# Three VectorE steps instead of four to turn fp64 weights into fp32, and full-height tail products

## The chip, the cores and the metric

One core of a Trainium2 chip runs one program: attention, a gated MLP over tokens and channels, and an MLP mixer, for a batch of four. The metric is the device time of one execution, in microseconds (us); lower is better. The engines are TensorE (PE; its weight loads are PEld), VectorE (DVE), ScalarE (ACT), GpSimd (POOL) and SyncE (SP, which issues the DMAs). Each works through its own list of instructions in order and waits on semaphores of the others.

## The reference, cut to what matters

```python
# attention: 4 batches, 8 heads, 1152 keys, 64 channels a head; queries are averaged in pairs (576)
scores = 1/sqrt(64) * q_pool @ k.T;  x = softmax(scores) @ v          # -> x: 4 x 576 x 512
# gated MLP
h = gelu(x @ w_in);  u, v = h[..., :512], h[..., 512:]
v_n = (v - mean(v)) / sqrt(var(v) + 1e-6) * g_ln
v_s = einsum('ts,bsd->btd', w_sg, v_n) + b_sg[None, :, None]          # 576 x 576 over tokens
x = x + (u * v_s) @ w_out
# mixer
h = maximum(x.T @ w_tok1, 0) @ w_tok2;  u = x + h.T                   # over tokens, 576 -> 256 -> 576
out = u + maximum(u @ w_ch1, 0) @ w_ch2
```

The weights `w_in`, `w_out`, `w_tok1`, `w_tok2`, `w_ch1` and `w_ch2` come as 64-bit floats and reach the kernel as 64-bit integers. `w_sg` is 32-bit.

## The kernel before

Every factor of a matmul is held as two fp32r tiles, a rounded high part and the rest (low), and a product is three matmuls: high by high, high by low, low by high (`products`, L203). The kernel has three stages in time.

*Attention* takes 16 pairs of a batch and two heads, some 32 us each. Its order on all engines is made by `Plan` (L62): every task has an engine, a duration, tasks that it follows and an urgency, and `run` places them one by one. PE's order is written out (`line`). DVE takes row maxima of scores (`mx`, L541), which PE waits for when its PSUM tiles run out; ACT takes exponentials (`e`, L592); POOL adds them up (`acc`, L598).

*The gated MLP* (`spatial`, L935) runs for each batch b: V (`psv`, L991), U (`psu`, L1057), the gate S over tokens (`pss`, `sg_mm`, L1075) in four blocks db, and the output product (`psz`/`pso`, L1099) of the batch before, after V. Each gate block is followed by a chain: DVE `gt` (L1084), POOL `gt` (L1087), ACT `g` (L1089), DVE `g` (L241). The order is that of the code; between its steps stand hooks, which `HOOKS` (L31) fills by name with other work. A "c" in it is one call of `feed.ops(1)`.

*The mixer* (`mixing`) has for each batch two blocks `psr` (`k1_mm`, L1256) with a relu split `r` into high (ACT, L1245) and low (DVE, L1246), then four blocks `psh` (L1266); after about 868 us come the channel products `psc` and `po`.

**The conversion.** A `Piece` (L251) is up to 128 x 512 weights: loaded by SP into `ws`, then turned into an fp32 tile `z` by bit operations on the upper word `top` and the lower word `low` of each number. `early` is two ACT instructions that make `d` (`wd`), the distance of the exponent from the middle; `step1` to `step4` are DVE instructions, the last of which takes numbers too small to zero by `d`. `high` (ACT, a cast) and `low_part` (POOL, a subtraction) split `z`. There are 42 pieces. Twelve are tasks of the plan (`conversion`); the other 30 go through `Feed`, whose generator `steps` yields after `step1` with `early`, after `step2` and after `step3`, and does the rest in a fourth call, so that a piece takes four calls of `ops`.

**The tail.** The 576 tokens are four tiles of 128 rows and a tail of 64. The tail tile of a token factor holds the high part in one half of its rows and the low part in the other, and the weight's high part stands in both halves, so that one 128-row matmul does two of the three products (`tail_products` leaves the third out). The matmul with the weight's low part (`sw` = 1) takes only the 64 rows with the high part: one matmul in 14, in `sg_mm` (4 batches x 4 blocks x 2 halves = 32) and in `k1_mm` (4 batches x 2 blocks = 8).

Of the kernel before, what the change touches and what calls it, by code (L numbers as in the profile page):

```python
# [11 lines left out]
F32 = mybir.dt.float32  # L12
F32R = mybir.dt.float32r
F16 = mybir.dt.float16
I32 = mybir.dt.int32
I64 = mybir.dt.int64
# [5 lines left out]
EXPMASK = 0x7F800000  # L22
# [125 lines left out]
def kernel(  # L148
# [16 lines left out]
    nc = tc.nc  # L165
# [20 lines left out]
    ident_r = const.tile([P, P], F32R, name="ident_r")  # L186
    ones = const.tile([P, P], F32, name="ones")
    m1024 = const.tile([P, 1], F32, name="m1024")
# [59 lines left out]
    class Piece:  # L248
# [17 lines left out]
        def early(self):  # L266
            self.d = d = self.cut(cvp.tile([P, 512], F16, tag="wd", name="wd", bufs=1))
            nc.scalar.activation(out=d, in_=self.top, func=AF.Abs, scale=2.0 ** -20)
            nc.scalar.activation(out=d, in_=d, func=AF.Abs, bias=m1024[:self.r])


        def step1(self):
            self.z = self.cut(cvp.tile([P, 512], F32, tag="wz", name="wz"))
            nc.vector.tensor_scalar(
                out=self.z.bitcast(I32), in0=self.top, scalar1=0x07FFFFFF, scalar2=3,
                op0=ALU.bitwise_and, op1=ALU.logical_shift_left)

        def step2(self):
            zi = self.z.bitcast(I32)
            nc.vector.scalar_tensor_tensor(  # L280
                out=zi, in0=self.low, scalar=29, in1=zi,
                op0=ALU.logical_shift_right, op1=ALU.bitwise_or)

        def step3(self):
            zi = self.z.bitcast(I32)
            nc.vector.scalar_tensor_tensor(  # L286
                out=zi, in0=self.top, scalar=-0x40000000, in1=zi,
                op0=ALU.bitwise_and, op1=ALU.bitwise_or)

        def step4(self):  # L290

            nc.vector.scalar_tensor_tensor(  # L292
                out=self.z, in0=self.d, scalar=127.0, in1=self.z, op0=ALU.is_le, op1=ALU.mult)
# [39 lines left out]
    class Feed:  # L333
# [16 lines left out]
        def steps(self, x):  # L350
            x.step1()
            x.early()
            yield
            x.step2()
            yield
            x.step3()
            yield
            x.step4()
            x.high()
            x.low_part()  # L360
            if x.away:
                for s in range(2):
                    x.send(s)
# [31 lines left out]
    def attention():  # L395
# [13 lines left out]
        for h in range(2):  # L409
            nc.vector.memset(f32(pick[D * h:D * h + 2]), 1.0)  # L410
        eps = keep.tile([P, 1], F32, name="eps", bufs=1)
# [204 lines left out]
        def sums(i, x):  # L616
            s = st[i][x]
            pt = bank()
            for h in range(2):
                nc.tensor.matmul(  # L620
                    pt[D * h:D * h + D, 0:TC], ones[:, 0:D], s.acc[:, h], start=True, stop=True)
            return pt
# [154 lines left out]
        for name, n in dict(ws=2, wd=1, wz=2, wn=1).items():  # L777
            plan.ring(name, n)
# [5 lines left out]
        def conversion(x, u):  # L784
            a = plan.add("SP", 0.05, lambda: x.load(nc.sync), after=[mark(u)], urgency=u - 20,
                         take=["ws"], land=4.0)
            d1 = plan.add("DVE", 1.0, x.step1, after=[a], urgency=u, take=["wz"])
            e = plan.add("ACT", 1.4, x.early, after=[a], urgency=u, take=["wd"])
            d2 = plan.add("DVE", 1.7, x.step2, after=[d1], urgency=u + 0.5)
            d3 = plan.add("DVE", 1.1, x.step3, after=[d2], urgency=u + 1)  # L790
            d4 = plan.add("DVE", 1.5, x.step4, after=[d3, e], urgency=u + 1.5,
# [138 lines left out]
    def spatial(fin, early):  # L930
# [221 lines left out]
        for b in range(B):  # L1152
# [15 lines left out]
            if last:  # L1168
# [6 lines left out]
                for j in range(JB):  # L1175
# [3 lines left out]
                todo.append(Piece(  # L1179
                    w_tok1[n0:T].rearrange("(a p) n -> p a n", p=TAIL),  # L1180
                    lambda: [x[r:r + TAIL, NTT - 1:NTT] for x, r in (
                        (L.wk1[0], 0), (L.wk1[1], 0), (L.wk1[0], TAIL))]))
# [18 lines left out]
    def mixing(L, fin):  # L1201
# [47 lines left out]
        def k1_mm(b, jb):  # L1249
# [113 lines left out]
    with tc.manual_schedule():  # L1363
        make_identity(nc, ident)
        nc.vector.tensor_copy(ident_r, ident)
        nc.vector.memset(ones, 1.0)
        nc.vector.memset(m1024, -1024.0)
        nc.scalar.copy(m1024, m1024)
        mixing(*spatial(*attention()))
# [31 lines left out]
```

## Time and profile before

| what | value |
|---|---|
| median of 3 runs | 1190.45 us (1186.25 to 1191.25) |
| the profiled execution | 1187.83 us, of which the span of instructions is 1186.0 us |
| busy over the span | PE 96%, PEld 79%, DVE 59%, ACT 38%, POOL 48% |
| granted TensorE clock, mean | 0.986 of full speed |
| mean of one conversion instruction, 128 x 512 | DVE 0.53, 0.88, 1.14 and 0.90 us; ACT 0.67 and 0.72 us |
| shortest and longest of step 3 (L286) | 0.42 and 1.83 us |

PE is busy nearly throughout, but a busy PE may be one whose matmuls start further apart than they need, and the rest of the question is where PE stands still and for whom. Rows of the timeline merge consecutive instructions of a line; the distance from the start of one row to the start of the next, divided by the count, is the time that one matmul takes of PE.

### The profile page before, as it was taken

Reading aid. Unit: us, or ns where it says so; the run is one execution under the profiler, and the core shown is the slowest. Engines: PE = TensorE matmul, PEld = TensorE weight load, DVE = VectorE, ACT = ScalarE, POOL = GpSimd, SP = SyncE. Lnnn points to the kernel's source line nnn. Section 1 sums busy time; section 2 is a strip of 40 time slices with the busy share of each in tenths; the row PEclk is TensorE's granted clock in tenths of the full one; section 3 lists DMA queues with packets and bytes.
Section 4 is the critical chain, followed back from the end, with each engine's and each line's share of the span. In section 5 each row is a group of like instructions: output and inputs, shape, how many; then the busy total and the mean of one; then the engine's idle time right before and its main releaser. Section 6 shows DMA issues by size and latency. Waiting matters only on the chain.

```text
span 1186.0 us, 22019 instructions
## 1 busy us (share of the span) xinstructions
PE 1139.7 (96%) x9249; PEld 938.8 (79%) x9249; DVE 700.2 (59%) x987; ACT 455.0 (38%) x821; POOL 571.7 (48%) x398
## 2 busy tenths in 40 slices
PE   5999999999999999998989999879999999999998
PEld 5777777777777777766879898867799888999887
DVE  5788888887676777746666666888841111212111
ACT  2355555454444555553434343445521111111111
POOL 2688888887777788783524342432240111110000
PEclk9999999999999999998999999989999999999999
DMA  8222234433334232117020201132230000000000
GB/s 180 42 66 69 78 79 107 120 81 79 80 91 99 72 83 67 57 54 252 29 79 20 88 18 54 54 98 89 89 143 19 19 19 10 18 10 19 18 19 18
DMA packets 81971, 79.68 MB, mean 67 GB/s; under 512 B 42192, under 2 KB 67024, under 8 KB 80592
## 3 DMA queue, kind: packets, MB, share of 16 engines
q1 hardware_dynamic: 81872, 78.28, 23.1%
q8 instruction: 72, 1.18, 0.4%
q14 instruction: 27, 0.22, 0.1%
HBM read 62.51 MB, written 15.76 MB: 66 GB/s over the span
## 4 chain that ended last, share of the span: by engine, by line
PE 74%; DVE 16%; ACT 4%; issue 3%; POOL 3%; DMA 0%; SPq 0%; DVEq 0%; POOLq 0%; ACTq 0%
PE sT L584 14%; PE psc L1319 13%; PE po L1339 13%; PE po L607 12%; PE s L534 10%; DVE mx L541 2%; PE pss L1075 2%; DVE wz L286 2%; PE psu L1057 2%; PE tt L483 2%; PE psz L1099 1%; POOL gt L1087 1%; DVE wz L280 1%; DVE wz L292 1%; PE pt L620 1%
## 5 line engine op out<-in xcount | busy, mean ns | idle before, releaser
L598 POOL TENSOR_TENSOR acc<-acc,e 128x576 f32<-128x576 f32 x224 | 322.2, 1439 | 75.2 <-ACT e L592 62.4
L541 DVE TENSOR_REDUCE mx<-s 128x2 f32<-128x768 f32 (+1 forms) x240 | 215.6, 945 | 90.9 <-PE s L534 90.9
L592 ACT ACTIVATE e<-sT 128x576 f32<-128x576 f32 x288 | 169.8, 651 | 96.0 <-PE sT L584 89.5
L584 PE MATMUL sT<-q,k 64*128 64x288 f32 x1728 | 167.7, 305 | 0.7 <-DVE mx L541 0.3
L584 PEld LDWEIGHTS sT<-q,k 64*128 64x128 f32 x1728 | 129.2, 186 | 43.5 <-DVE mx L541 16.6
L607 PE MATMUL po<-e,vn 128*64 128x288 f32 x1152 | 160.8, 414 | 0.0
L1319 PEld LDWEIGHTS psc<-x,w 128*128 128x128 f32 x1296 | 155.9, 189 | 0.7
L1319 PE MATMUL psc<-x,w 128*128 128x256 f32 x1296 | 156.3, 282 | 0.0
L1339 PE MATMUL po<-w,gc 128*128 128x512 f32 x648 | 153.3, 396 | 0.0
L534 PE MATMUL s<-k,q 64*128 64x384 f32 (+1 forms) x1440 | 147.7, 346 | 3.2 <-ACT k L516 1.1
L1339 PEld LDWEIGHTS po<-w,gc 128*128 128x128 f32 x648 | 120.8, 188 | 28.9
L1245 ACT ACTIVATE gc<-psc 128x256 fp32r<-128x256 f32 x108 | 41.6, 385 | 244.2 <-PE psc L1319 244.2
L534 PEld LDWEIGHTS s<-k,q 64*128 64x128 f32 (+1 forms) x1440 | 112.2, 179 | 21.0 <-ACT e L592 3.4
L607 PEld LDWEIGHTS po<-e,vn 128*64 128x64 f32 x1152 | 74.3, 136 | 57.5 <-issue 17.3
L1246 DVE SCALAR_TENSOR_TENSOR gc<-psc,gc 128x256 fp32r<-128x256 f32 x108 | 45.9, 425 | 108.1 <-ACT gc L1245 108.1
L237 POOL TENSOR_SCALAR x<-xT 128x1024 fp32r<-128x1024 f32 x9 | 9.8, 1088 | 198.6 <-PE psc L1319 198.1
L1346 DVE TENSOR_TENSOR ob<-po,us 128x512 f32<-128x512 f32 x18 | 12.4, 692 | 145.7 <-PE po L1339 145.7
L584 PE MATMUL sT<-nmT,pick 64*128 64x288 f32 x576 | 85.6, 292 | 0.0
L631 DVE RECIPROCAL pt<-pt 128x288 f32<-128x288 f32 x32 | 62.7, 1961 | 26.2 <-ACT pt L627 26.1
L1075 PE MATMUL pss<-wsg,vn 128*128 128x288 f32 x448 | 73.0, 310 | 3.8 <-POOL vn L241 3.8
L1075 PEld LDWEIGHTS pss<-wsg,vn 128*128 128x128 f32 x448 | 62.4, 188 | 14.0 <-issue 4.8
L241 POOL TENSOR_TENSOR vn<-gv,vn 128x512 fp32r<-128x512 f32 (+1 forms) x20 | 27.1, 1367 | 72.2 <-ACT vn L1041 69.8
(111 smaller groups left out, 1491.1 us busy)
## 6 DMA issues: line engine op xcount, KB each, us to landing
ws<-in_moe_w_ch_dram SPq DMA_DIRECT2D x24, 512.0 KB, 3.6
qn<-in_q_dram SPq DMA_DIRECT2D x32, 288.0 KB, 5.1
kn<-in_k_dram SPq DMA_DIRECT2D x32, 288.0 KB, 4.3
vn<-in_v_dram SPq DMA_DIRECT2D x32, 288.0 KB, 3.3
out_dram<-ob SPq DMA_DIRECT2D x18, 256.0 KB, 2.0
ws<-in_moe_w_in_dram SPq DMA_DIRECT2D x8, 512.0 KB, 4.8
ac<-ws SPq DMA_DIRECT2D x16, 256.0 KB, 2.4
w<-ac SPq DMA_DIRECT2D x4, 1024.0 KB, 8.7
```

What stands on the lines that cost most here:

```text
L534: nc.tensor.matmul(ps[0:m, h, 0:KC], flat(c.q[x])[r, t * P:t * P + m], c.k[y][r, cs], start=(n == 0), stop=(n == 2))
L541: nc.vector.tensor_reduce(out=mx[i % 2][0:m, t, :, g], in_=ps[0:m, :, 0:KC], axis=AX.X, op=ALU.max, negate=True)
L584: nc.tensor.matmul(ps[:, h, 0:TC], left, right, start=(n == 0), stop=(n == 3))
L592: nc.scalar.activation(out=s.e[j], in_=ps[:, :, 0:TC], func=AF.Exp)
L598: eng.tensor_tensor(out=s.acc, in0=s.e[0] if j == 1 else s.acc, in1=s.e[j], op=ALU.add)
L607: nc.tensor.matmul(s.po[D * h:D * h + D, 0:TC], c.vn[:, h, j], s.e[j][:, h], start=(j == 0), stop=(j == J - 1))
L631: nc.vector.reciprocal(out=s.den, in_=s.den)
L1075: nc.tensor.matmul(ps[:, ch, 0:TC], V[sx][r, ti, db * P:(db + 1) * P], L.ws[sw][r, ti, ch * TC:(ch + 1) * TC], start=first, stop=end)
L1245: nc.scalar.activation(out=h_, in_=ps, func=AF.Relu)
L1246: nc.vector.scalar_tensor_tensor(out=l_, in0=ps, scalar=0.0, in1=f32(h_), op0=ALU.max, op1=ALU.subtract)
L1319: nc.tensor.matmul(ps, WC1[f // 4][sw][:, cc, (f % 4) * P:(f % 4 + 1) * P], u[sx][:, cc], start=first, stop=end)
L1339: nc.tensor.matmul(pos[tt], g[sx][:, f, tt * P:(tt + 1) * P], WC2[f // 4][sw][:, f % 4], start=(f == 0 and n == 0), stop=(f == NF - 1 and ...
```

## The change

The three DVE steps now are: `step1` shifts the upper word with one bit flipped, `step2` masks the result and ORs in `y`, `step3` takes the minimum with the largest fp32 and multiplies by `d`. `y` (new tile `wy`) holds the top three bits of the lower word and is made by one ACT instruction (`early`); `d` is now the sign of a scaled upper word, made by two ACT instructions (`signs`, with the function Sign). Both are called in the piece's first call, after `step1`. The piece still takes four calls: the third now holds the last DVE step, and the fourth only the split. In the plan the low bits stand ahead of the signs, with durations 0.7 and 1.4. The tail matmuls with the weight's low part take all 128 rows, and for the mixer POOL sets the lower 64 rows of that tile to zero. The constants `ident_r` and `ones` are made inside the attention stage, and `m1024` is gone.

```diff
         def early(self):
+            self.y = y = self.cut(cvp.tile([P, 512], I32, tag="wy", name="wy", bufs=1))
+            nc.scalar.activation(out=y, in_=self.low.bitcast(U32), func=AF.Copy,
+                                 scale=2.0 ** -29 * (1 - 2.0 ** -20), bias=-0.5 + 2.0 ** -22)
+
+        def signs(self):
             self.d = d = self.cut(cvp.tile([P, 512], F16, tag="wd", name="wd", bufs=1))
-            nc.scalar.activation(out=d, in_=self.top, func=AF.Abs, scale=2.0 ** -20)
-            nc.scalar.activation(out=d, in_=d, func=AF.Abs, bias=m1024[:self.r])
+            nc.scalar.activation(out=d.bitcast(I16), in_=self.top.bitcast(F32), func=AF.Copy,
+                                 scale=TINY)
+            nc.scalar.activation(out=d, in_=d.bitcast(I16), func=AF.Sign)
...
             nc.vector.tensor_scalar(
-                out=self.z.bitcast(I32), in0=self.top, scalar1=0x07FFFFFF, scalar2=3,
-                op0=ALU.bitwise_and, op1=ALU.logical_shift_left)
+                out=self.z.bitcast(I32), in0=self.top, scalar1=0x08000000, scalar2=3,
+                op0=ALU.bitwise_xor, op1=ALU.logical_shift_left)
...
             nc.vector.scalar_tensor_tensor(
-                out=zi, in0=self.low, scalar=29, in1=zi,
-                op0=ALU.logical_shift_right, op1=ALU.bitwise_or)
+                out=zi, in0=zi, scalar=0x7FFFFFFF, in1=self.y,
+                op0=ALU.bitwise_and, op1=ALU.bitwise_or)
...
         def step3(self):
-            zi = self.z.bitcast(I32)
             nc.vector.scalar_tensor_tensor(
-                out=zi, in0=self.top, scalar=-0x40000000, in1=zi,
-                op0=ALU.bitwise_and, op1=ALU.bitwise_or)
-
-        def step4(self):
-            nc.vector.scalar_tensor_tensor(
-                out=self.z, in0=self.d, scalar=127.0, in1=self.z, op0=ALU.is_le, op1=ALU.mult)
+                out=self.z, in0=self.z, scalar=HUGE, in1=self.d, op0=ALU.min, op1=ALU.mult)
...
             x.step1()
             x.early()
+            x.signs()
             yield
             x.step2()
             yield
             x.step3()
             yield
-            x.step4()
             x.high()
             x.low_part()
...
-            e = plan.add("ACT", 1.4, x.early, after=[a], urgency=u, take=["wd"])
...
+            y = plan.add("ACT", 0.7, x.early, after=[a], urgency=u, take=["wy"])
+            e = plan.add("ACT", 1.4, x.signs, after=[a], urgency=u + 1, take=["wd"])
...
-                    r = high_rows(b, ti) if sw else slice(0, P)
                     nc.tensor.matmul(
-                        ps[:, ch, 0:TC], V[sx][r, ti, db * P:(db + 1) * P],
-                        L.ws[sw][r, ti, ch * TC:(ch + 1) * TC], start=first, stop=end)
+                        ps[:, ch, 0:TC], V[sx][:, ti, db * P:(db + 1) * P],
+                        L.ws[sw][:, ti, ch * TC:(ch + 1) * TC], start=first, stop=end)
...
+                def tail_dst():
+                    nc.gpsimd.memset(f32(L.wk1[1][TAIL:P, NTT - 1:NTT]), 0.0)
+                    return [x[r:r + TAIL, NTT - 1:NTT] for x, r in (
+                        (L.wk1[0], 0), (L.wk1[1], 0), (L.wk1[0], TAIL))]
...
-                r = slice(0, TT[ti][1] if sw else P)
                 nc.tensor.matmul(
-                    ps, wk1[sw][r, ti, jb * P:(jb + 1) * P], c.y[sx][r, ti],
+                    ps, wk1[sw][:, ti, jb * P:(jb + 1) * P], c.y[sx][:, ti],
                     start=first, stop=end)
```

What this moves is seen best on DVE. In the first gate stage (batch 0), from the first block's chain to the second's; `wz` is the piece's fp32 tile, `gt` and `g` the gate's. Before:

```order
L280 SCALAR_TENSOR_TENSOR wz<-ws,wz 128x512
L1084 SCALAR_TENSOR_TENSOR gt<-pss,g_half,b_bc 128x2x288
L286 SCALAR_TENSOR_TENSOR wz<-ws,wz 128x512
L241 TENSOR_TENSOR g_7607<-gt,g_7606 128x576
L292 SCALAR_TENSOR_TENSOR wz<-wd,wz 128x512
L274 TENSOR_SCALAR wz<-ws 128x512
```

The same stretch now:

```order
L289 SCALAR_TENSOR_TENSOR wz<-wz,wy 128x512
L1090 SCALAR_TENSOR_TENSOR gt<-pss,g_half,b_bc 128x2x288
L295 SCALAR_TENSOR_TENSOR wz<-wz,wd 128x512
L241 TENSOR_TENSOR g_7616<-gt,g_7615 128x576
L282 TENSOR_SCALAR wz<-ws 128x512
```

The step that completes the piece stood behind `g` and now stands ahead of it, and one step is gone.

In the last gate stage (batch 3), one block's chain to the next. Before:

```order
L1084 SCALAR_TENSOR_TENSOR gt<-pss,g_half,b_bc 128x2x288
L280 SCALAR_TENSOR_TENSOR wz<-ws,wz 128x512
L286 SCALAR_TENSOR_TENSOR wz<-ws,wz 128x512
L292 SCALAR_TENSOR_TENSOR wz<-wd,wz 128x512
L241 TENSOR_TENSOR g_7607<-gt,g_7606 128x576
L274 TENSOR_SCALAR wz<-ws 128x512
```

The same stretch now:

```order
L1090 SCALAR_TENSOR_TENSOR gt<-pss,g_half,b_bc 128x2x288
L289 SCALAR_TENSOR_TENSOR wz<-wz,wy 128x512
L295 SCALAR_TENSOR_TENSOR wz<-wz,wd 128x512
L241 TENSOR_TENSOR g_7616<-gt,g_7615 128x576
L282 TENSOR_SCALAR wz<-ws 128x512
```

Three conversion steps between `gt` and `g` have become two.

In the mixer's first batch, around the two relu splits `r`. Before:

```order
L274 TENSOR_SCALAR wz<-ws 128x512
L280 SCALAR_TENSOR_TENSOR wz<-ws,wz 128x512
L286 SCALAR_TENSOR_TENSOR wz<-ws,wz 128x512
L1246 SCALAR_TENSOR_TENSOR r_9780<-psr,r_9779 128x512
L292 SCALAR_TENSOR_TENSOR wz<-wd,wz 128x512
L1246 SCALAR_TENSOR_TENSOR r_9780<-psr,r_9779 128x512
```

The same stretch now:

```order
L282 TENSOR_SCALAR wz<-ws 128x512
L289 SCALAR_TENSOR_TENSOR wz<-wz,wy 128x512
L295 SCALAR_TENSOR_TENSOR wz<-wz,wd 128x512
L1254 SCALAR_TENSOR_TENSOR r_9811<-psr,r_9810 128x512 x2
L241 TENSOR_TENSOR y_9851<-pty,y_9850 128x512 x3
```

The last conversion step has moved from between the two `r` to ahead of both. PE's matmuls keep their order in all these stages.

## Rows read from the trace of the kernel before

**Rows 1.** Windows by stage: length, each engine's busy us (instructions), clock, DMA.
```profile
35.00:535.00 500.00, 497.87 (x5228) 367.27 (x5226) 381.81 (x451) 252.85 (x450) 408.25 (x275) 1.00 0.31 79
...
600.00:800.00 200.00, 182.64 (x1159) 166.38 (x1157) 137.07 (x220) 80.63 (x129) 78.07 (x61) 0.96 0.17 57
800.00:868.00 68.00, 63.81 (x364) 52.53 (x364) 59.05 (x86) 34.67 (x60) 19.10 (x13) 1.00 0.25 78
```

**Rows 2.** Timeline of PE: start, us, instructions, [idle before <-releaser].
```profile
635.51 18.15 PE L1075 MATMUL pss<-wsg,vn 128*128 128x288 f32 x112
653.50 14.32 PE L991 MATMUL psv<-w,x 128*128 128x512 f32 x60
667.65 3.35 PE L1099 MATMUL pso<-g,wo 128*128 128x288 f32 x24
...
684.07 12.89 PE L1057 MATMUL psu<-x,w 128*128 128x288 f32 x96
696.79 18.09 PE L1075 MATMUL pss<-wsg,vn 128*128 128x288 f32 x112
...
783.34 4.09 PE L1099 MATMUL pso<-g,wo 128*128 128x288 f32 x18 [3.56 <-ACT g L1089]
...
817.22 7.47 PE L1256 MATMUL psr<-y,x 128*128 128x512 f32 x28
824.53 1.69 PE L1238 MATMUL pty<-ident,xT 128*128 128x128 f32 x12
```

**Rows 3.** Groups by form, conversion: count | busy us, mean ns of one | idle before.
```profile
L286 DVE SCALAR_TENSOR_TENSOR wz<-ws,wz 128x512 int32<-128x512 int32 x38 | 43.3, 1139 | 0.5
...
L292 DVE SCALAR_TENSOR_TENSOR wz<-wd,wz 128x512 f32<-128x512 f16 x38 | 34.2, 899 | 1.2
L280 DVE SCALAR_TENSOR_TENSOR wz<-ws,wz 128x512 int32<-128x512 int32 x38 | 33.2, 875 | 0.9
...
L269 ACT ACTIVATE wd<-wd,m 128x512 f16<-128x512 f16 x38 | 27.5, 724 | 1.2
...
L268 ACT ACTIVATE wd<-ws 128x512 f16<-128x512 int32 x38 | 25.5, 671 | 0.0
...
L274 DVE TENSOR_SCALAR wz<-ws 128x512 int32<-128x512 int32 x38 | 20.0, 526 | 0.1
```

**Rows 4.** Waits of PE from 600 to 872 us: total, times, longest.
```profile
PE psv L991 <- ACT x L384: 3.1, 1, 3.1
...
PE psz L1099 <- DVE gv L927: 1.8, 1, 1.8
...
PE pso L1099 <- ACT g L1089: 7.9, 2, 4.4
PE pss L1075 <- POOL vn L241: 2.9, 1, 2.9
PE psh L1266 <- ACT r L1245: 2.7, 4, 1.0
PE psh L1266 <- DVE r L1246: 1.3, 1, 1.3
```

**Rows 5.** Timeline of the last gate stage on DVE, ACT and POOL.
```profile
773.64 0.81 DVE L1084 SCALAR_TENSOR_TENSOR gt<-pss,g_half,b_bc 128x576 f32<-128x576 f32 x1
...
775.09 1.77 DVE L286 SCALAR_TENSOR_TENSOR wz<-ws,wz 128x512 int32<-128x512 int32 x1
776.96 0.69 DVE L292 SCALAR_TENSOR_TENSOR wz<-wd,wz 128x512 f32<-128x512 f16 x1
...
780.19 0.80 DVE L1084 SCALAR_TENSOR_TENSOR gt<-pss,g_half,b_bc 128x576 f32<-128x576 f32 x1
...
777.68 0.62 ACT L302 CAST x<-wz 128x512 fp32r<-128x512 f32 x1 [4.38 <-DVE wz L292]
...
774.60 1.71 POOL L1087 TENSOR_TENSOR gt<-gt,gu 128x576 f32<-128x576 f32 x1 [1.82 <-DVE gt L1084]
```

**Rows 6.** Groups by form, the one load of ACT's function table.
```profile
L1368 ACT ACT_TABLE_LOAD x1 | 1.3, 1283 | 0.7 <-PEq L1385 0.7
```

More of the change, by code (lines that the diff above doesn't have):

```diff
@@ L14 @@
 F16 = mybir.dt.float16
+I16 = mybir.dt.int16
 I32 = mybir.dt.int32
+U32 = mybir.dt.uint32
 I64 = mybir.dt.int64
@@ L20 @@
 PSUM = bass.MemoryType.PSUM
-EXPMASK = 0x7F800000
+HUGE = float(np.finfo(np.float32).max)
+TINY = 2.0 ** 14 / 1.0625
 C1 = float(np.float32(np.sqrt(2.0 / np.pi)))
@@ L185 @@
     ident = const.tile([P, P], F32, name="ident")
-    ident_r = const.tile([P, P], F32R, name="ident_r")
-    ones = const.tile([P, P], F32, name="ones")
-    m1024 = const.tile([P, 1], F32, name="m1024")
     xT = const.tile([P, CC, NT], F32, name="xT")
@@ L410, in attention @@
             nc.vector.memset(f32(pick[D * h:D * h + 2]), 1.0)
+        ident_r = ld.tile([P, P], F32R, name="ident_r")
+        nc.vector.tensor_copy(ident_r, ident)
+        ones = keep.tile([P, D], F32, name="ones", bufs=1)
+        nc.vector.memset(ones, 1.0)
         eps = keep.tile([P, 1], F32, name="eps", bufs=1)
@@ L620, in sums @@
                 nc.tensor.matmul(
-                    pt[D * h:D * h + D, 0:TC], ones[:, 0:D], s.acc[:, h], start=True, stop=True)
+                    pt[D * h:D * h + D, 0:TC], ones, s.acc[:, h], start=True, stop=True)
             return pt
@@ L776, in attention @@
             tasks(i)
-        for name, n in dict(ws=2, wd=1, wz=2, wn=1).items():
+        for name, n in dict(ws=2, wd=1, wy=1, wz=2, wn=1).items():
             plan.ring(name, n)
@@ L786, in conversion @@
                          take=["ws"], land=4.0)
-            d1 = plan.add("DVE", 1.0, x.step1, after=[a], urgency=u, take=["wz"])
-            e = plan.add("ACT", 1.4, x.early, after=[a], urgency=u, take=["wd"])
-            d2 = plan.add("DVE", 1.7, x.step2, after=[d1], urgency=u + 0.5)
-            d3 = plan.add("DVE", 1.1, x.step3, after=[d2], urgency=u + 1)
-            d4 = plan.add("DVE", 1.5, x.step4, after=[d3, e], urgency=u + 1.5,
+            d1 = plan.add("DVE", 0.9, x.step1, after=[a], urgency=u, take=["wz"])
+            y = plan.add("ACT", 0.7, x.early, after=[a], urgency=u, take=["wy"])
+            e = plan.add("ACT", 1.4, x.signs, after=[a], urgency=u + 1, take=["wd"])
+            d2 = plan.add("DVE", 1.3, x.step2, after=[d1, y], urgency=u + 1, give=[("wy", y)])
+            d4 = plan.add("DVE", 1.3, x.step3, after=[d2, e], urgency=u + 1.5,
                           give=[("wd", e)] + ([] if x.away else [("ws", a)]))
@@ L1178, in spatial @@
                                       dst([w[:, 0:n0 // P] for w in L.wk1], P, c)))
[L1179 to L1182, printed above, removed]
+                def tail_dst():
+                    nc.gpsimd.memset(f32(L.wk1[1][TAIL:P, NTT - 1:NTT]), 0.0)
+                    return [x[r:r + TAIL, NTT - 1:NTT] for x, r in (
+                        (L.wk1[0], 0), (L.wk1[1], 0), (L.wk1[0], TAIL))]
+                todo.append(Piece(w_tok1[n0:T].rearrange("(a p) n -> p a n", p=TAIL), tail_dst))
                 for j in range(3):
@@ L1364 @@
         make_identity(nc, ident)
[L1365 to L1368, printed above, removed]
         mixing(*spatial(*attention()))
```

## The prediction

> **What bounds the kernel now.** I read the busy time by stage first, then the timeline of PE for how far apart its matmuls start, then the waits of PE, and last the chains that those waits lead back to. By stage, PE is busy for 497.87 of 500 us of attention, for 182.64 of the 200 us from 600 on, and for 63.81 of 68 us of the mixer's token part, where DVE is busy for 59.05 [rows 1]. So PE sets the time nearly everywhere, and what can be won is of two kinds: matmuls that start further apart than they must, and the waits of PE in the MLP and the mixer.
>
> The first kind shows where the halved matmuls are. The gate stage of batch 1 has 112 matmuls of 288 columns and runs without a pause from 635.51 to 653.50, 17.99 us; batch 2's U stage, 96 matmuls of the same width, takes 12.72 us, 0.1325 each [rows 2]. At that rate 112 would take 14.84. The gate stage is 3.15 us longer and has 8 matmuls with 64 rows: 0.39 us each. In the mixer 28 matmuls of 512 columns take 7.31 us, against 28 x 0.2358 = 6.60 at the rate of the 60 matmuls `psv` (14.15 us), which is 0.71 for 2 of them, 0.35 each [rows 2]. Two stages of different width give nearly the same excess per 64-row matmul, so it goes with the change of height and not with the columns.
>
> The second kind: PE waits 3.1 us for an ACT split of x after gate stage 0, 1.8 for DVE's gelu after stage 1, 2.9 for POOL's normalized v before stage 3, 7.9 for ACT's g after it, and 2.7 + 1.3 for the relu splits in the mixer [rows 4]. The chain behind the 7.9 is in the rows of the last gate stage: `gt` on DVE at 773.64 and the next one only at 780.19, a period of 6.55 us although PE needs about 4.5 per block. Within it step 3 takes 1.77 and step 4 0.69, and ACT's cast, idle 4.38 us for step 4, stands ahead of ACT's g [rows 5].
>
> **The change part by part.** *Tail matmuls.* 32 in the gate and 8 in the mixer take 128 rows: 4 x 3.15 + 4 x 0.71 = 15.4 us less of PE time. A matmul of 128 rows in the same place costs the common 0.13 or 0.24; the smallest saving is none, if the excess is not from the height, the largest 15.4. I take 15.4, since it repeats at both widths. Whether it reaches the end depends on the waits behind each stage.
>
> The Trainium skill speaks of this twice, in opposite directions: "TensorEngine Tiling (Array Packing)", Theoretical Speedup, gives contractions of at most 64 rows up to twice the speed when tiled, and Key Properties says that a change of tiling mode drains TensorE. By the first, full height would win nothing (that is the fourth rival); by the second, each lone 64-row matmul pays on the way in and out. The excess of 0.39 us [rows 2] is on the side of the second.
>
> *DVE.* Four steps average 0.53 + 0.88 + 1.14 + 0.90 = 3.44 us a piece [rows 3]. Gone is one of three SCALAR_TENSOR_TENSOR; the two that stay have new operations and one contiguous operand instead of a strided one, which the trace doesn't show: between the 0.69 of an undisturbed one and the 1.77 of one beside a running POOL instruction [rows 5]. I take old prices for them, and for the one removed 0.69 in a chain, 0.97 (the mean of the three) in sum: 42 x 0.97 = 41 us less of DVE, of which most lies beside PE work.
>
> The Trainium skill, "SBUF — State Buffer", Who interferes with whom, says that a DVE instruction with two SBUF inputs is blocked for the whole of a GpSimd instruction that reads SBUF. Step 3 started at 775.09 and ended 0.55 us after POOL's `gt` (774.60 for 1.71) [rows 5], which agrees. By this rule the step after the removed one inherits the block, so that a chain gains 0.69 and not 1.77.
>
> *ACT.* One more instruction per piece, priced as its neighbours at 0.67 (0.72 as the other end) [rows 3]: 28 us in all. It is hidden where ACT waits anyway, as for step 4 above (4.38 us idle), and costs up to 0.67 where an x split or a relu stands behind it. New waits: step 2 for `y`, step 3 for the signs, up to 0.67 + 0.67 + 0.72 = 2.06 us after the piece's first call. Behind them on DVE stand `gt`, relu lows and, in attention, row maxima.
>
> *Order.* The last step is now one call earlier. Where ACT's cast follows, z is ready when ACT comes to it, and g, x splits and relus behind the cast go at once. POOL's zeroing is one small instruction where POOL is idle. SP issues the same DMAs; a few in attention change places, and PE does not wait for DMAs there.
>
> Now by place, each with its bounds. A chain gains 0.79 by the first block (two tail matmuls sooner), and 0.69 to 1.8 for each conversion in it.
> - Stage 0: three conversions, 0.79 + 2.1 = 2.9 to 6.2. All that PE could use is 3.15 + 3.1. I take 4 (0 to 6.25).
> - Stage 1: three conversions, the same; PE could use 3.15 + 1.8. I take 4 (0 to 5).
> - Stage 2: two conversions, and `y` stands ahead of x splits that POOL does before its `gt`: 0.79 + 1.4 - 0.67 = 1.5 to 3.6. I take 2 (0 to 3.6).
> - Stage 3: 0.79 + 2.1 by the chain, and 1 of the wait for v, whose cast stands behind a conversion's. I take 4 (0 to 3.15 + 2.9 + 7.9 = 14).
> - Mixer, token part: 2.8 of matmuls, and 2.7 of the 4.0 us of waits, since the cast that held up the second relu is done before it. Three pieces a batch need some 3.4 us each by ACT (2.06, then a DVE step of 0.69, then the cast 0.62), as much as before by DVE, so not all goes. I take 5.5 (2.8 to 6.8).
> - Attention: 2.1 us of idle in all [rows 1], some of it behind conversions. I take 1 (from 4 lost, by new waits, to 2.1 won).
>
> The sum is 4 + 4 + 2 + 4 + 5.5 + 1 = 20.5 us. The profiled execution took 1187.83, so 1167.3; the median of the runs is 2.6 us above that execution, and with it the sum gives 1170.0. I forecast 1169. All lower ends together give 1.2 us lost, all upper ends 37.7 won: 1150 to 1192.
>
> **The rivals.** *The waits eat PE's gain.* ACT's extra instruction takes the place of DVE's, the chains stay as long as they were, and PE comes earlier to the same waits. Then only the mixer's 2.8, about 0.8 a stage by the earlier first block and perhaps 2 of the order remain: 8 us, 1181. For it: four of five gate and mixer waits are for ACT or DVE chains [rows 4]. Against: ACT's idle 4.38 us before the cast [rows 5], three times what it gets to do.
>
> *More than the sum.* After the long waits PE is slow: 18 matmuls from 783.34 took 4.09 us, 0.227 each against 0.1325 [rows 2]. If the waits shrink, this goes too, 1.7 us there, and steps save 1.8 rather than 0.69 in the chains: about 30 us, 1159.
>
> *Attention waits for the new steps.* Twelve pieces, each with DVE held for up to 2.06 us while row maxima stand behind it: if PE felt it all, 12 x 2.06 = 25 us would be lost against 19.5 won elsewhere, about 1195. For it: PE and DVE are tight there. Against: in the order the two kinds of ACT instructions stand well ahead, and ACT is busy for only 252.85 of 500 us [rows 1].
>
> *Not the height.* If the 0.39 us stay with 128 rows, the chains and relu waits alone give about 9 us: 1180.
>
> *Slower: table loads.* Sign is a function that the kernel has not used so far. If it lies in another table than the exponential and tanh, each piece pays two loads of 1.283 us [rows 6], 42 x 2.57 = 108 us, on ACT in front of exponentials that PE and POOL wait for: 1169 + 108 = 1277. It decides from 8 such pieces on. Against: ACT's list of the changed kernel has a single table load, at its start, as before.
>
> **How the numbers follow.** Forecast, 1163 to 1176: 0.60. Waits eat the gain, 1177 to 1186: 0.17. More, 1152 to 1162: 0.12. Attention waits: 0.04. Not the height: 0.05. Table loads: 0.02. The range 1157 to 1182 holds the forecast whole, about half of the case in which waits eat the gain and of the one with more, and the one of the height: 0.8. A difference under 0.5%, 6 us, can't be told from none here, so faster means below 1184.5: 0.60 + 0.12 + 0.13 of the 0.17 + 0.04 of the 0.05 = 0.89. Slower, above 1196.4, is the table loads and a bad case of attention, 0.03; the same is what is left, 0.08.
>
> **What would show it.** After: no matmul row with 64 rows at the gate or `psr` lines; gate stage 1 from its first matmul to the next stage's first in 14.9 us instead of 17.99, the mixer's pair of blocks in 6.6 instead of 7.31. DVE with three groups on `wz` and some 40 us less; ACT with 28 us more and one table load. The wait for g after stage 3 at 4 to 6 instead of 7.9, the waits at `psh` under 2, the one for x after stage 0 under 3. The forecast is wrong if gate stages keep their length, if PE's waits from 600 to 870 grow by over 5 us, or if attention takes over 3 us longer, with DVE waiting for `wy` or `wd`.

## The result, and the profile after

The changed kernel takes 1161.3 us (median, 1160.8 to 1162.2) where the kernel before, timed beside it on the same chip, takes 1189.8: a ratio of 0.9766, 95% interval 0.9743 to 0.9789. The forecast was 1169, the range 1157 to 1182. The profiled executions are 1187.83 and 1161.53 us, 26.3 us apart; the rest of the difference of the medians is that the profiled execution of before was among its faster ones.

The three stretches of [rows 1], after (length, then PE, PEld, DVE, ACT, POOL busy, clock, DMA):

```profile
35.00:535.00 500.00, 499.51 (x5245) 368.42 (x5244) 369.52 (x440) 260.53 (x466) 409.25 (x276) 1.00 0.31 79
600.00:800.00 200.00, 186.60 (x1252) 175.78 (x1252) 140.02 (x224) 97.67 (x164) 78.89 (x64) 0.97 0.20 63
800.00:868.00 68.00, 65.99 (x437) 60.30 (x436) 42.24 (x67) 33.66 (x64) 22.40 (x16) 1.00 0.32 117
```

In the same 200 us from 600 on PE now starts 1252 matmuls where it started 1159; they are not quite the same ones, since the stages now come earlier. The timeline of PE in the changed kernel, the places of [rows 2]:

```profile
628.51 15.00 PE L1081 MATMUL pss<-wsg,vn 128*128 128x288 f32 x112
643.35 8.55 PE L998 MATMUL psv<-w,x 128*128 128x512 f32 x36
...
655.64 4.01 PE L998 MATMUL psv<-w,x 128*128 128x512 f32 x16 [1.35 <-POOL x L241]
...
757.24 0.69 PE L1105 MATMUL pso<-g,wo 128*128 128x288 f32 x4
761.79 0.53 PE L1105 MATMUL pso<-g,wo 128*128 128x288 f32 x2 [3.86 <-ACT g L1095]
766.20 4.27 PE L1105 MATMUL pso<-g,wo 128*128 128x288 f32 x18 [3.88 <-ACT g L1095]
...
798.35 6.70 PE L1263 MATMUL psr<-y,x 128*128 128x512 f32 x28
804.88 1.03 PE L1246 MATMUL pty<-ident,xT 128*128 128x128 f32 x8
```

Gate stage 1 lasts 643.35 - 628.51 = 14.84 us instead of 17.99, a pair of mixer blocks 6.53 instead of 7.31. But there is now a wait behind gate stage 1, the one behind stage 2 has grown, and the two waits for g are as long in sum as they were. The waits of PE from 572 to 876 us, against [rows 4], which start at 600 (from 572 on the kernel before has 3.6 us for ACT's x and 3.8 for vn):

```profile
PE pso L1105 <- ACT g L1095: 7.7, 2, 3.9
PE psv L998 <- ACT x L387: 4.0, 3, 1.9
PE pss L1081 <- POOL vn L241: 2.2, 2, 1.8
PE psv L998 <- POOL x L241: 1.3, 1, 1.3
PE psh L1273 <- DVE r L1254: 1.1, 1, 1.1
PE psh L1273 <- ACT r L1253: 0.7, 2, 0.5
```

The groups of the conversion, against [rows 3] and [rows 6]:

```profile
L289 DVE SCALAR_TENSOR_TENSOR wz<-wz,wy 128x512 int32<-128x512 int32 x38 | 38.5, 1013 | 6.0 <-ACT wy L269 3.7 <-DVE wz L282 0.5
L295 DVE SCALAR_TENSOR_TENSOR wz<-wz,wd 128x512 f32<-128x512 f32 x38 | 38.2, 1006 | 1.4
L269 ACT ACTIVATE wy<-ws 128x512 int32<-128x512 uint32 x38 | 25.6, 672 | 0.4 <-DMA ws<-in_moe_w_in_dram 0.4
L275 ACT ACTIVATE wd<-ws 128x512 int16<-128x512 f32 x38 | 25.2, 662 | 0.0
L282 DVE TENSOR_SCALAR wz<-ws 128x512 int32<-128x512 int32 x38 | 24.9, 655 | 0.5 <-DMA ws<-in_moe_w_in_dram 0.4
L277 ACT ACTIVATE wd<-wd 128x512 f16<-128x512 int16 x38 | 24.0, 631 | 1.2
...
L499 ACT ACT_TABLE_LOAD x1 | 1.3, 1283 | 0.7 <-PEq L1388 0.7
```

DVE is busy for 667.0 us instead of 700.2, ACT for 473.6 instead of 455.0, and there is one table load, as before. The last gate stage, one block's `gt` to the next, against [rows 5]:

```profile
751.14 0.81 DVE L1090 SCALAR_TENSOR_TENSOR gt<-pss,g_half,b_bc 128x576 f32<-128x576 f32 x1
...
752.65 1.73 DVE L295 SCALAR_TENSOR_TENSOR wz<-wz,wd 128x512 f32<-128x512 f32 x1
...
757.30 0.81 DVE L1090 SCALAR_TENSOR_TENSOR gt<-pss,g_half,b_bc 128x576 f32<-128x576 f32 x1
...
763.05 0.81 DVE L1090 SCALAR_TENSOR_TENSOR gt<-pss,g_half,b_bc 128x576 f32<-128x576 f32 x1
```

The period is 6.16 us, and the next one is 5.75; before they were 6.92 (from a `gt` at 766.72) and 6.55. So each lost about one bare step, and the long step beside POOL's `gt` is still there.

By place, from the starts of PE's stages in both traces:

| place (start of a stage to start of a later one) | before | after | won | forecast (bounds) |
|---|---|---|---|---|
| attention to gate stage 0 | 574.85 | 573.90 | 0.95 | 1 (-4 to 2.1) |
| stage 0 and the V behind it | 35.23 | 29.17 | 6.06 | 4 (0 to 6.25) |
| stage 1, V, output product | 48.56 | 43.97 | 4.59 | 4 (0 to 5) |
| stage 2 and V | 29.88 | 29.53 | 0.35 | 2 (0 to 3.6) |
| batch 3's output, U, stage 3, last output | 70.14 | 65.12 | 5.02 | 4 (0 to 14) |
| mixer, token part | 71.41 | 64.83 | 6.58 | 5.5 (2.8 to 6.8) |
| channel MLP to the end | 317.78 | 315.02 | 2.76 | nothing |

The rows add up to the 26.3 us, but for U and output products in between, which did not change. All but the last lie within the prediction's bounds. That says where the time was won, not what won it.

### The profile page after: what moved, and what is told of

Its sections match the earlier page's. It is cut to its first block, busy times and chain, and to the rows that moved or that the text cites. A ratio compares the mean times of both kernels' runs of the same rounds, so it can differ in the third digit from the quotient of the medians.

```text
span 1159.7 us, 22044 instructions
## 1 busy us (share of the span) xinstructions
PE 1118.9 (96%) x9249; PEld 935.3 (81%) x9249; DVE 667.0 (58%) x944; ACT 473.6 (41%) x862; POOL 570.4 (49%) x399
## 4 chain that ended last, share of the span: by engine, by line
PE 79%; DVE 9%; ACT 4%; POOL 3%; issue 3%; DMA 1%; SPq 0%; POOLq 0%; DVEq 0%; ACTq 0%
PE sT L591 15%; PE psc L1326 13%; PE po L614 13%; PE po L1346 13%; PE s L541 11%; PE psz L1105 3%; PE psu L1064 2%; PE tt L490 2%; POOL gt L1093 2%; PE pt L627 1%; DVE mx L548 1%; PE psv L998 1%; PE pso L1105 1%; DVE wz L289 1%; DVE wz L295 1%
## 5 line engine op out<-in xcount | busy, mean ns | idle before, releaser
L1346 PE MATMUL po<-w,gc 128*128 128x512 f32 x648 | 150.7, 393 | 0.0
L1081 PE MATMUL pss<-wsg,vn 128*128 128x288 f32 x448 | 60.5, 295 | 2.2 <-POOL vn L241 2.2
L1081 PEld LDWEIGHTS pss<-wsg,vn 128*128 128x128 f32 x448 | 59.6, 188 | 2.6 <-POOL vn L241 2.6
```

What stands on the lines that cost most here:

```text
L1081: nc.tensor.matmul(ps[:, ch, 0:TC], V[sx][:, ti, db * P:(db + 1) * P], L.ws[sw][:, ti, ch * TC:(ch + 1) * TC], start=first, stop=end)
L1346: nc.tensor.matmul(pos[tt], g[sx][:, f, tt * P:(tt + 1) * P], WC2[f // 4][sw][:, f % 4], start=(f == 0 and n == 0), stop=(f == NF - 1 and ...
```

## The experiments

**Each part alone.** The first theory was the prediction's: the tails free 15.4 us of PE, the old chains keep a part of it, the conversion's shorter chains give the rest. The first kernel is the one before with this alone (the mixer's in the same way):

```diff
-                    r = high_rows(b, ti) if sw else slice(0, P)
-                        ps[:, ch, 0:TC], V[sx][r, ti, db * P:(db + 1) * P],
-                        L.ws[sw][r, ti, ch * TC:(ch + 1) * TC], start=first, stop=end)
+                        ps[:, ch, 0:TC], V[sx][:, ti, db * P:(db + 1) * P],
+                        L.ws[sw][:, ti, ch * TC:(ch + 1) * TC], start=first, stop=end)
```

> The kernel before, with the 40 tail products over 128 rows and nothing else changed (the old four conversion steps). If the prediction's split holds (PE's time of 15.4 us goes, but the old chains stay, so that PE comes earlier to the same waits), each gate stage lasts 14.9 us instead of 17.99 and the mixer's pair of blocks 6.6 instead of 7.31, while PE's waits from 600 to 870 us grow by some 7 us; the time is 7 to 10 us less than before, 1180 to 1183. The rival, that PE's time alone counts, gives 15 us less, 1174 to 1175, with the waits as they were. The rival that the excess is not from the height gives no change.

The second is the changed kernel with these lines turned back.

> The changed kernel, with the tail products by the weights' low part over 64 rows again: the conversion and the constants' new places alone. If waits had eaten a part of what the tails give, the two parts help each other: the tails alone give 7 to 10 and this one gives 12 to 16 (1174 to 1178), and their sum falls short of the 28.5 us of both. If PE's time alone counts, this one gives 13 us and the tails 15, and they add up. Gate stages stay at 17.9 to 18 us in either case.

| | old conversion | new conversion |
|---|---|---|
| 64-row tails | 1190.7 | 1164.3, ratio 0.9786 (0.9763 to 0.9808) |
| 128-row tails | 1193.9, ratio 1.0032 (1.0019 to 1.0045) | 1161.3, ratio 0.9766 (0.9743 to 0.9789) |

The stages' lengths came as expected, and the sum of the parts does fall short of both together; every expected time was missed. The tails alone win nothing, they cost 0.2 to 0.45%; the conversion alone wins 26.4 us, and the tails add 3.0 to that (2.4 by the ratios, each to the kernel before as timed beside it; the ratios' intervals overlap, the single runs of the two kernels don't). The stretch from the first gate matmul to the first channel matmul (the same 1663 matmuls, but for missing records), one row a kernel: before, tails alone, conversion alone, both.

```profile
574.85:868.22 293.37, 270.91 (x1663) 239.56 (x1662) 210.25 (x326) 125.89 (x205) 110.26 (x84) 0.97 0.19 63
```

```profile
575.74:874.47 298.73, 262.93 (x1662) 244.04 (x1661) 211.04 (x326) 125.51 (x205) 109.44 (x84) 0.94 0.19 61
```

```profile
573.14:847.41 274.27, 265.75 (x1663) 237.49 (x1661) 191.57 (x298) 138.92 (x235) 109.55 (x84) 0.98 0.21 67
```

```profile
573.90:844.68 270.78, 253.10 (x1662) 235.29 (x1661) 191.07 (x297) 138.61 (x235) 109.57 (x85) 0.98 0.21 68
```

Length less PE's busy time is PE's idle time: 22.5, 35.8, 8.5 and 17.7 us. With the tails alone gate stages 0 to 2 do last 14.8 to 15.2 us, yet PE's busy time falls by 8.0 only, not 15.4, since the granted clock falls from 0.97 to 0.94 of full speed, and idle time grows by 13.3. With the new conversion the same edit takes 12.7 us off PE's busy time and adds 9.2 of idle. So little of PE's time in the gate and the mixer's blocks was on the path in either kernel. PE behind the first gate stage, tails alone:

```profile
590.98 8.55 PE L991 MATMUL psv<-w,x 128*128 128x512 f32 x36
604.96 4.51 PE L991 MATMUL psv<-w,x 128*128 128x512 f32 x12 [5.43 <-ACT x L384]
609.30 2.94 PE L1098 MATMUL pso<-g,wo 128*128 128x288 f32 x21
```

and conversion alone:

```profile
592.14 11.48 PE L998 MATMUL psv<-w,x 128*128 128x512 f32 x48
603.46 3.34 PE L1106 MATMUL pso<-g,wo 128*128 128x288 f32 x24
```

With the old chains PE comes 3 us earlier to a wait that is 2.3 longer than before (3.1), and then runs 12 matmuls at 0.36 us each instead of the 0.236 of an undisturbed stretch. In the kernel before they took 0.37 behind the shorter wait, so what the tails change here is the length of the wait and not the slow matmuls behind it. With the new chains and the slow tails there is no wait at all. The costliest place of the tails alone is the mixer's end:

```profile
862.62 0.66 PE L1266 MATMUL psh<-x,r 128*128 128x288 f32 x3 [1.03 <-ACT r L1246]
866.76 7.87 PE L1266 MATMUL psh<-x,r 128*128 128x288 f32 x43 [3.48 <-DVE r L1247]
874.47 1.70 PE L1319 MATMUL psc<-x,w 128*128 128x256 f32 x13
```

There the wait for DVE grew from 1.3 us [rows 4] to 3.5, and 43 matmuls take 0.179 us each, where the same 43 took 0.136 before. The granted clock from 861.2 to 874.5 us, the waits included, is 0.74. In pieces, the wait and what follows it:

```profile
863.30:866.70 3.40, 0.00 (x0) 0.00 (x0) 3.37 (x3) 0.00 (x0) 2.26 (x1) 0.63 0.00 0
866.70:870.00 3.30, 3.24 (x13) 3.24 (x14) 1.16 (x3) 0.00 (x0) 0.00 (x0) 0.50 0.03 5
```

Behind the wait 13 matmuls fill 3.3 us at half the clock; from 872 on it is 1.00 again.

**Is it the change of height?** The kernel before, with the gate's two 64-row matmuls of a block put next to each other:

```diff
+                seq = [(x[2:], bool(x[4] and x[2] == NTT - 1)) for x in tail_products()]
+                seq.sort(key=lambda x: x[1], reverse=bool(ch))
+                for k, ((ti, sx, sw), _) in enumerate(seq):
...
```

> The kernel before, with the gate's 64-row matmul put last in the first half's group and first in the second half's, so that the two of a block stand next to each other; number and height of all matmuls stay. If the 0.39 us are the price of going from 128 rows to 64 and back, a block pays it once and not twice: gate stages last 16.4 us instead of 17.99, and 64-row rows come in pairs. If a 64-row matmul is slow by itself, the stages stay at 18.0. Of the 6.3 us that PE would win, 2 to 5 should reach the time (1185 to 1188), by the waits behind the stages.

Gate stage 1, from its first row to the next stage's:

```profile
635.92 16.56 PE L1077 MATMUL pss<-wsg,vn 128*128 128x288 f32 x112
652.32 10.42 PE L991 MATMUL psv<-w,x 128*128 128x512 f32 x44
```

16.40 us, as the expectation's first case has it: the 0.39 us are paid for each trip to 64 rows and back, not for each matmul. The time did not follow, as the expectation of 1185 to 1188 had it: 1189.7, ratio 0.9997 (0.9983 to 1.001). PE's idle time in the stretch grew from 22.5 to 27.8 us. It is the second kernel in which PE's gate time is shortened with the old conversion and nothing comes of it.

**Number of steps, or their place?** The new conversion has one step less, and the last one stands a call earlier. Two kernels part these. In the first the three steps stay, and the last goes back to the fourth call:

```diff
-            x.step3()
             yield
+            yield
+            x.step3()
             x.high()
```

> The changed kernel, with its last conversion step of the feed's pieces put back into the piece's fourth call, right ahead of the cast, where the old last step stood; three DVE steps as now, and the 12 pieces of the plan untouched. If the number of steps makes the gain, the time stays at 1160 to 1163. If it is the place (the piece is complete before the gate's g and the mixer's relus, so that ACT's cast finds it done), most of the 26 us of the conversion goes back: 1172 to 1186, with the waits for x, g and r of the kernel before.

The second has the four old steps and the old two ACT instructions, with the fourth step in the third call:

```diff
             x.step3()
+            x.step4()
             yield
-            x.step4()
             x.high()
```

> The changed kernel, with the old four DVE steps and the old two ACT instructions, but the fourth step in the piece's third call, right behind the third one, so that a piece is complete a call earlier than before; the tails over 128 rows and the constants' places are the changed kernel's. If the place makes the gain, 1163 to 1170, since a chain is longer by only one bare step of 0.69 us. If it is the number, it is the kernel with the new tails alone, less 2.8 us of the channel MLP: 1188 to 1192.

They take 1177.0 us (0.9889, 0.9874 to 0.9904) and 1181.8 us (0.9928, 0.9913 to 0.9942). The first lies where its expectation put the place, the second between its two cases, so neither alone does it. "Number" here stands for the whole new conversion, its third ACT instruction and the operand `y` in place of the strided `low` included. Both are measured against the tails alone (1193.9), less what the channel MLP gets by the place of its tiles (below): 2.8 us in the kernel with the late step and in the changed one, 4.0 in the one with four steps, whose channel chunks come 34.42 us apart. So the number wins 14, the place 8, and both together 29.8: each theory was a part of it, and the remaining 7.7 come only with both. They are waits in the main: in the stretch from the first gate matmul to the first channel matmul PE is idle for 35.8 us with the tails alone, 27.5 with the late step, 32.4 with four early ones and 17.7 in the changed kernel. The places differ. With the late step there are waits for x behind stages 0 to 2 of 5.3, 2.0 and 4.0 us, longer than in the kernel before, while the wait for g stays at 7.7. ACT there, behind stage 0:

```profile
599.96 0.67 ACT L1095 CAST g<-gt 128x576 fp32r<-128x576 f32 x1 [2.43 <-POOL gt L1093]
602.06 0.62 ACT L305 CAST ws<-wz 128x512 fp32r<-128x512 f32 x1 [1.43 <-DVE wz L295]
602.58 0.92 ACT L387 CAST x<-xT 128x512 fp32r<-128x512 f32 x2
```

The split of x stands behind the piece's cast, and that waits 1.43 us for a last step which DVE does only after the low part of g. With four early steps it is the wait for g that is long (9.9 us) and, in the mixer, those for DVE's relu; DVE at the mixer's end:

```profile
853.68 2.71 DVE L288 SCALAR_TENSOR_TENSOR wz<-ws,wz 128x512 int32<-128x512 int32 x1
856.50 0.69 DVE L294 SCALAR_TENSOR_TENSOR wz<-wd,wz 128x512 f32<-128x512 f16 x1
857.11 0.68 DVE L1253 SCALAR_TENSOR_TENSOR r<-psr,r 128x512 fp32r<-128x512 f32 x1
```

The relu for which PE waits 4.27 us stands behind a step that took 2.71.

**The channel MLP, whose code did not change.** In the compiled programs, by their address lists, the tiles of its hidden layer (`gc`), the stationary operand of `po`, begin at 63136 bytes of each partition before and at 62080 after, 32 bytes past a multiple of 64 and on one. Two tests of that. The first puts 32 bytes among the constants, the second only ahead of these tiles:

```diff
+    pad = const.tile([P, 8], F32, name="pad")
+    nc.vector.memset(pad, 0.0)
     xT = const.tile([P, CC, NT], F32, name="xT")
...
         gp = pool(ctx, "gc", 1)
+        pad = gp.tile([P, 8], F32, name="pad")
+        nc.gpsimd.memset(pad, 0.0)
```

> The changed kernel, with an unused tile of 32 bytes a partition among the constants, which moves all tiles allocated after it on that side by 32 bytes and changes no other instruction than its one memset. In the channel MLP, whose code did not change, the po matmuls took 229 ns instead of 233 in the changed kernel; their stationary operand stands there at a multiple of 64 bytes instead of an odd multiple of 32. If the place in SBUF makes the difference, po goes back to 233 and the time rises by 2.5 to 3.5 us for this stage and the mixer's token part; attention, whose operands on that side go the other way (from odd multiples to even ones), may win something, 0 to 5 us. If it is something else (the instructions' order, the DMAs), po stays at 229 and the time within 1 us.

> The changed kernel, with 32 bytes a partition (and one memset by POOL) ahead of the channel MLP's hidden tiles alone, the stationary operand of po, which so stand at odd multiples of 32 bytes as before the change; no other tile moves. If their place sets the rate of po, a chunk's period goes from 34.56 to 34.87 us and the time rises by 2.8 us, with nothing changed before the channel MLP. If it is another tile that had moved with them (xT, the output tiles), the period stays at 34.56 and the time within 0.5 us of 1161.

The 72 `po` matmuls of a chunk, before, after, and with the second pad:

```profile
886.20 17.05 PE L1339 MATMUL po<-w,gc 128*128 128x512 f32 x72
```

```profile
897.23 16.74 PE L1346 MATMUL po<-w,gc 128*128 128x512 f32 x72
```

```profile
897.31 17.04 PE L1348 MATMUL po<-w,gc 128*128 128x512 f32 x72
```

With either pad 17.04; the kernels take 1164.3 and 1164.9 us, 3.0 and 3.6 more than the changed kernel, which was timed in another session. The second pad moves those tiles alone, so it is the place of the stationary tiles: 0.31 us a chunk, 2.8 us in nine. The kernel with four early steps has them at 62144, the next multiple of 64, and is faster still, 16.43 us from the first `po` to the next stage, where the changed kernel takes 16.58 and the one before 16.88. Its other tiles on that side moved too, by the same 64 bytes, so that this last 0.15 us is due to the stationary tiles isn't shown; if it is, being on a multiple of 64 is not the whole rule. The mixer's blocks, which I had also put down to it, stay at 6.54 with the first pad; their 0.78 us are the two tails alone, 0.39 each. That attention gains by the first pad isn't shown: its next stage began 0.7 us sooner, but its two largest groups of matmuls take 0.303 and 0.414 us in the mean in both.

**The gate's chain itself.** A block's `gt`, POOL's `gt`, ACT's g and DVE's low part take some 4.0 us without any conversion between them (in gate stage 0 of the changed kernel from a `gt` at 590.14 to the DVE instruction behind g at 594.19), more than the 3.71 of its matmuls, and the next block's `gt` is issued behind all of it. If that chain is what the stages wait for, issuing the next block's `gt` ahead of this block's g should give PE's gain back:

```diff
+            open_ = None
             for db in range(CC):
-                run(sg_mm, sg_act, f"{b}S{db}", b, db)
+                name = f"{b}S{db}"
+                ps = sg_mm(b, db, lambda: hook(name + "m"))
+                hook(name + "a")
+                it = sg_act(b, db, *ps)
+                next(it)               # gt on DVE and POOL
+                if open_:
+                    next(open_, 0)     # g of the block before
+                hook(name + "e")
+                if db == CC - 1:
+                    next(it, 0)
+                open_ = it
+                hook(name + "z")
```

> The changed kernel, with the gate's blocks overlapping: gt of block db + 1 (DVE and POOL) is issued before ACT's g and DVE's low part of g of block db, in place of behind them; no instruction is added or taken away. In the changed kernel a block's chain of DVE, POOL, ACT and DVE takes 4.0 us bare and 5.8 to 6.2 with conversion steps in it, against 3.71 us of matmuls. If that chain is what PE waits for behind the gate stages, the waits of 1.9, 1.6 and 1.9 us for x go and that of 7.7 for g falls to 2 to 4, and the granted clock recovers: 1149 to 1155. If the conversion's load on DVE, ACT and POOL is the limit, the waits stay within 1 us each and the time within 2 us of 1161.

1153.4 us, 0.9689 (0.9673 to 0.9706): faster than both kernels, 7.9 us less than the changed one. DVE and PE in it:

```profile
582.90 0.80 DVE L1090 SCALAR_TENSOR_TENSOR gt<-pss,g_half,b_bc 128x576 f32<-128x576 f32 x1
583.63 1.12 DVE L241 TENSOR_TENSOR g<-gt,g 128x576 fp32r<-128x576 f32 x1
...
586.38 0.81 DVE L1090 SCALAR_TENSOR_TENSOR gt<-pss,g_half,b_bc 128x576 f32<-128x576 f32 x1
```

```profile
589.12 12.02 PE L998 MATMUL psv<-w,x 128*128 128x512 f32 x48
600.98 3.34 PE L1105 MATMUL pso<-g,wo 128*128 128x288 f32 x24
...
754.03 0.85 PE L1105 MATMUL pso<-g,wo 128*128 128x288 f32 x2 [2.77 <-ACT g L1095]
757.38 4.69 PE L1105 MATMUL pso<-g,wo 128*128 128x288 f32 x18 [2.50 <-ACT g L1095]
```

`gt` follows `gt` in 3.5 us, and the waits for x behind stages 0 to 2 are gone. The wait for g fell to 5.3, not to the 2 to 4 that I expected. The clock did not recover either: in the stretch of the token stages of the profiled execution it is 0.97, with PE busy for 255.0 us, 1.9 more than in the changed kernel, so the gain is in PE's idle time, 9.5 us instead of 17.7. Two more kernels use this order as a probe: overlapping blocks with 64-row tails, and overlapping blocks in the kernel before.

> The kernel with overlapping gate blocks, with the tail products by the weights' low part over 64 rows again. In the changed kernel the tails bring 2.9 us beyond the conversion, while PE's matmuls became 15.4 us shorter. If the gate's chain is what swallows the rest, then without it (blocks overlapping) the tails are worth close to what PE gets: 4 x 3.15 in the gate less about 3 in the last stage, where waits remain, and 2.8 in the mixer, so 10 to 15 us: 1163 to 1168. If it is lost otherwise, the difference stays near 3 us: 1156 to 1157.

> The kernel before, with the gate's blocks overlapping as in the overlapped kernel and nothing else: four conversion steps, 64-row tails. If the gate's chain sets the stages, overlapping takes the waits for x and gv (3.1, 1.8 and 0.5 us with their slow clock) and part of the 7.9 for g: 1178 to 1184, while the mixer keeps its waits for r. If the conversion's own steps hold DVE, POOL and ACT, the time stays within 3 us of 1190.

1163.2 us (0.9777, 0.9759 to 0.9794) and 1181.1 us (0.9925, 0.9907 to 0.9943). The tails, worth -3.2 us with the old conversion and 3.0 with the new, are worth 9.8 once blocks overlap, at the lower edge of the expected 10 to 15. In the stretch of the token stages they now take 11.0 us off PE's busy time and add only 2.2 of idle time. And the kernel before wins 9 us by the order alone, within what was expected. Both agree with a chain that swallowed PE's gain.

Two attempts at more won nothing. In one ACT's g keeps its old place and only the low part moves:

```diff
             nc.scalar.copy(two(L.g[0][:, db]), g)
+            yield
             sub(nc.vector, two(L.g[1][:, db]), g, two(f32(L.g[0][:, db])))
```

> The kernel with overlapping gate blocks, but ACT's g is issued in its old place, right after its own block's conversion calls, and only DVE's low part of g comes after the next block's gt. In the overlapped kernel ACT's g of one block stood behind the cast and the three ACT instructions of the next piece. If that is what keeps 5.3 us of waits for g behind the last gate stage, they fall to 2 to 4 and the time to 1148 to 1152. If ACT then holds the next block's splits, nothing is won: 1153 to 1156.

1158.0 us (0.9734, 0.9712 to 0.9755), 4.6 slower than with both moved and above either expectation: the wait for g stays at 5.3 us, and those for x are back (1.7 and 1.6), since the splits stand behind a g that waits for POOL. The other:

> The kernel with overlapping gate blocks, and an unused tile of 32 bytes a partition (with one memset) ahead of the other tiles of attention's left pool, which puts its tiles of v and of the exponentials at multiples of 64 bytes, as they were before the change, while the channel MLP keeps its own. The kernel with 32 bytes among the constants had attention 0.7 us shorter and the channel MLP 2.8 us longer. If the place does it, attention is 0.5 to 0.9 us shorter than in the kernel with overlapping blocks, po stays at its 34.56 us a chunk period, and the time is 0.7 us less. If not, the two are the same within 0.3 us.

1153.6 us (0.9697, 0.968 to 0.9713), the same; attention ended 0.3 us sooner, which isn't told apart from nothing. `po` took 34.56 a chunk period.

## Why the prediction was right in its time and not in its split

- *Where the time fell.* 1161.3 us is not in the forecast's own 1163 to 1176 but in "more than the sum", 1152 to 1162, which had a chance of 0.12. That rival wanted shorter waits, a faster clock behind them and steps that save 1.8 us. PE's idle time did shrink, from 22.5 to 17.7 us, but the 18 matmuls behind the wait for g, on which the rival counted, still take 4.1 us, and the chains of stage 3 lost about 0.8 us a block. The rival's time came true, its mechanism only in part.
- *The PE term.* In the gate it came out to the hundredth: 14.84 us a stage, 0.39 us for each lone 64-row matmul. The mixer's term was a little small, 6.53 us and not 6.60, 0.39 us each and not 0.35: the rate of 0.2358 us taken from `psv` is not that of `psr`, which now takes 6.53 / 28 = 0.233. "TensorEngine Tiling (Array Packing)", Key Properties, of the Trainium skill says that a change of tiling mode drains TensorE; the trace agrees, since neighbours of one height halved the price. The prediction had said that it depends on the waits behind each stage whether this reaches the end, and still let about 6 us of it through (0.79 a stage and 2.8 in the mixer). Measured, it was a loss of 3.2 us with the old chains and 3.0 won on top of the new.
- *The step that failed* is "a chain gains 0.79 by the first block, and 0.69 to 1.8 for each conversion in it", with the low ends taken in the long stages. Without the tails the conversion won 26.4 us, 2.8 of them by the tiles' place, so 23.6 against the 14.5 that are left of the sum without the tails. What was mis-sized was not the step, which is 0.69 bare as before, but that number and place win more together than their sum: a piece complete before `g` frees ACT's queue (x, relus) as well as DVE's, and of 29.8 us they win 14 and 8 alone.
- *The clock* was left at nothing in the forecast and stood only in the rival with more than the sum. It works in both directions: with the same matmuls PE is busy for 262.9 us with the old conversion and 253.1 with the new one, 9.8 us by the granted clock alone (0.94 and 0.98).
- *The waits eat PE's gain* was given 0.17 as an outcome of the whole change. As a mechanism it is right for the tails and even too mild, since the clock makes it a loss; the conversion's shorter chains outweigh it.
- *Stage 3.* The wait for g was to shrink to 4 to 6 us and is 7.7. From the stage's start to the last g 4.8 us went (30.6 to 25.8), but PE's own stage became 4.3 shorter (21.1 to 16.9, of it 1.1 of the wait for v): both ends moved together.
- *Stage 2*, 0.35 instead of 2: its 3.1 us of PE went into a wait for x that rose from 0.5 to 1.9, and into 12 `psv` matmuls behind it that took 4.2 us and not 3.
- *DVE's block*: step 3 beside POOL's `gt` still takes 1.73 us, and the period lost 0.8, not the 1.7 of a long step. "SBUF — State Buffer", Who interferes with whom, in the Trainium skill says that a DVE instruction with two SBUF inputs contends with a GpSimd one that reads SBUF; the trace agrees here too. DVE fell by 33 us, not 41: the shift takes 0.66 in the mean instead of 0.53 (13 of its 38 full-size instructions took over 0.55 us, 6 before), and the two steps that stay take 1.01 instead of the 0.97 that the old three had. ACT rose by 18.6, not 28: by the rows the new instruction does cost 27.6 us, but the two others take 4.9 less than before, and the other 4 us aren't accounted for.
- *Attention, table loads, height*: 0.95 us to the first gate stage for the 1 forecast, one table load, and 0.39 us that did go with the height.

That 1161 fell into the range rests on terms that erred in opposite ways. A time that comes out right doesn't prove the sum.

## What to carry to other kernels

Before pricing an engine's saving, ask which chain that engine meets next: here 15.4 us of PE were worth -3, 3 or 10 us, by the state of the chain behind. A short conversion step in an in-order queue is worth most by what stands behind it, so count what it lets go on each engine, and try its place and its number apart. And where a chain of one block is nearly as long as the block's matmuls, issue the next block's first step before this block's last one; that was worth 8 to 9 us in either kernel.

## What the runs showed of the hardware

- A wait of PE can cost more than its length: with the tails alone, behind a wait of 3.5 us at the mixer's end, the granted clock was 0.50 for 3.3 us (the lower of its two levels, 1.2 of 2.4 GHz), and 43 matmuls took 7.7 us where they took 5.8 behind a wait of 1.3. Over the token stages the same matmuls kept PE busy for 253.1 us with 17.7 us of idle time and for 262.9 with 35.8.
- The 72 `po` matmuls of a chunk take 16.88 us when their stationary tiles begin 32 bytes past a multiple of 64 (at 62112) and 16.58 on one (at 62080), with no other tile moved. At 62144, in a kernel where other tiles moved too, they take 16.43. No other position was tried, attention showed no such effect, and the rule behind it is open.
- A DVE shift with one SBUF input, 0.41 us when POOL is idle, took up to 1.5 in the changed kernel while POOL ran. The section on who interferes with whom in "SBUF — State Buffer" of the Trainium skill says that an instruction with one SBUF input meets GpSimd only in a mode that takes both of DVE's ports, and that this kind of instruction can enter such a mode; the trace agrees.
